# Gated spectral/MLP layer with gradients: two quarters of w1 loaded during the output pass into tiles of their own, and a new order of products where the gradient of x begins

## Chip, cores and metric

One core of a Trainium2 chip. The metric is the device time of one execution in microseconds (us), from the first to the last instruction and what lies around them; the median of several executions is compared. The layer has 2048 rows, model width D = 1024 and hidden width F = 3584, all in bf16.

## What is computed

The forward layer mixes a Fourier filter and an MLP with a squared ReLU by a gate for each row, and the call returns its output and the gradients of eight of its inputs:

```python
g = sigmoid((x * gate_w).sum(-1, keepdims=True))
a = irfft2(rfft2(x) * (w_r + 1j * w_i), s=(S, D))      # spectral branch
h = einsum("bsd,df->bsf", x, w1) + b1
r = where(h > 0, h, 0)
b = einsum("bsf,fd->bsd", r * r, w2) + b2              # MLP branch, fed from B_x
out = g * a + (1 - g) * b
out, vjp = jax.vjp(f, A_x, A_w_r, A_w_i, B_w1, B_b1, B_w2, B_b2, gate_w)
return (out, *vjp(grad_out))
```

The part that matters here is the last one. The output needs h2 = (relu h)² times w2. The kernel's second output is computed from dh (the gradient at the hidden layer) times the transpose of w1, plus the spectral and the gate's part of the gradient; the text calls it the gradient of x. Both are products of 2048 × 3584 by 3584 × 1024.

## The kernel before

The kernel runs in three stages: the hidden layer and its gradient (`mlp_in`), the gradients of w2 and w1 (`mlp_grads`), the output and gradient of x (`mlp_out`); the Fourier work is spread between the matmuls of the first stages. h2 and dh are kept transposed in DRAM scratch (`h2T_scr`, `dhT_scr`). All that follows is in `mlp_out`.

**Blocks and products.** `mlp_out` walks over NB = 8 blocks of 256 rows, first for the output ("h", from `h2T_scr`) and then for the gradient of x ("d", from `dhT_scr`). A block is loaded into the tile `even` or `odd` by its number, in two halves of the 28 chunks of 128 (`lo`: chunks 0 to 13, `hi`: 14 to 27). Apart from the first two blocks of "h", a block is multiplied by Strassen's scheme in Winograd's form: the block and the 3584 × 1024 matrix are cut in 2 × 2 quarters, and seven products take the place of eight. Each product (`p1` to `p7`) is a chain of 14 matmuls of 128 × 128 by 128 × 512 into one PSUM bank. The quarters of the block are a11, a21 (both in `lo`), a12, a22 (both in `hi`).

**The sums.** `Block.sums` makes four sums of a block's quarters on VectorE (S3 = a11 − a21; S1 = a21 + a22, in place of a21; S2 = S1 − a11; S4 = a12 − S2). `right` makes the four sums of the matrix's quarters (T1 = b12 − b11, T2 = b22 − T1, T4 = b21 − T2, T3 = b22 − b12), each over 128 × 7168 elements. The products need: p1 a11·b11, p2 a12·b21, p3 S4·b22, p4 a22·T4, p5 S1·T1, p6 S2·T2, p7 S3·T3. p1, p6, p7 and p4 follow one another in the bank X, each copied out by ScalarE before the next adds to it; p5 and p3 share the bank V.

**Where the matrices lie.** For "h" the quarters of w2 are in `w2L` (`cL`) and `w2R` (`cR`), T1, T2, T4 in the three tiles `wT1`, `wT2`, `wT4`, and T3 in place of `cR[:, lo]`. For "d" the quarters of w1 must be transposed: `quarter` issues seven DMA transposes from SyncE for one of them. One quarter has its own tile (`w1q`) and comes early. The other three are put where w2 lay: b12 in `cL[:, lo]`, b22 in `cL[:, hi]`, b21 in `wT2`; so each can start only when the last block of "h" is done with that place.

**What sets the order.** [...] Inside `mlp_out` the order on TensorE, VectorE and ScalarE is the order of the calls (`pe`, `dve` and `act` chain each instruction behind the one before). `ld` issues a DMA from SyncE's queue, `st` from GpSimd's; the scheduler sorts the two queues by when their work becomes due, and a DMA that has to wait for its buffer holds back all that stands behind it on its queue.

**Lines that the steps touch.** L1124 and L1163 allocate the rows of the incoming gradient and of x (3 buffers); L1145 and L1168 the scaled row `od`/`gd`; L1140 to L1153 are the tail of an output tile (`close`: add, then a product with a row sum, L1142, into `ot`; `put`: subtract and store); `prepare_x` (L1166) makes the spectral and gate part of a gradient tile and adds to `gacc`; L1318 to L1360 is the loop over blocks of "h"; L1363 to L1401 is the order where "d" begins; L1403 to L1422 the loop over its later blocks; L1423 to L1430 the end.

Of the kernel before, what the change touches and what calls it, by code (L numbers as in the profile page):

```python
# [10 lines left out]
P = 128  # L11
# [128 lines left out]
def kernel(  # L140
# [667 lines left out]

    def column_sums(sb_pool, acc, tag):

        tr_ = sb_pool.tile([P, D], FP32, name="tr_", tag=tag, bufs=1)
        nc.vector.transpose(out=tr_[:], in_=acc[:])
        part = sb_pool.tile([P, 32], FP32, name="part", tag="part")
        nc.vector.reduce_sum(out=part[:], in_=tr_[:].rearrange("p (b r) -> p b r", r=32), axis=mybir.AxisListType.X)
        return part

    def sums_out(sb_pool, ps_pool, tag, part, dst, bufs=2):

        pr = ps_pool.tile([32, 32], FP32, name="prow", tag=tag, bufs=bufs)
        mm(pr[:], lhsT=part[:], rhs=sel[:], start=True, stop=True)  # L820
        row = sb_pool.tile([32, 32], BF16, name="row", tag="row")
        nc.vector.tensor_copy(out=row[:], in_=pr[:])
        st(out=dst.rearrange("(b c) -> b c", c=32), in_=row[:])


    def mlp_grads():
# [255 lines left out]
    def mlp_out():  # L1082
# [4 lines left out]
        wp, wps = pool("w1p")  # L1087
        q0 = wp.tile([P, KH, H], BF16, name="w1q", tag="w1q")
        wb, wbs = pool("m3")
# [5 lines left out]
        row = lambda name, dt=FP16, bufs=2, tag=None: wb.tile([P, D], dt, name=name, tag=tag or name, bufs=bufs)  # L1095
        a_, go, na, v, cu, od, ot, blks = ({} for _ in range(8))
        B, Bx = {}, {}
# [25 lines left out]
        def fetch_g(t):  # L1123
            go[t] = row("go3", BF16, 3)  # L1124
            (ld if t < NT - 2 else st)(out=go[t][:], in_=go_perm[t])

# [10 lines left out]
        def close(t):  # L1137
            c_ = slice(t, t + 1)
            d_, g_ = cu.pop(t), go.pop(t)
            ot[t] = row("ot", BF16)  # L1140
            dve(V(out=d_[:], in0=d_[:], in1=v.pop(t)[:], op=ALU.add))
            dve(nc.vector.tensor_tensor_reduce(  # L1142
                out=ot[t][:], in0=d_[:], in1=g_[:], scale=1.0, scalar=0.0,
                op0=ALU.mult, op1=ALU.add, accum_out=bGo[:, c_],
            ))  # L1145
            od[t] = row("od", bufs=1)
            act(nc.scalar.mul(out=od[t][:], in_=d_[:], mul=omg[:, c_]))
            dve(STT(out=dsc[:, c_], in0=bGo[:, c_], scalar=-1.0, in1=gpg[:, c_], op0=ALU.mult, op1=ALU.mult))

        def put(t):  # L1150
            o_ = ot.pop(t)
            dve(V(out=o_[:], in0=od.pop(t)[:], in1=na.pop(t)[:], op=ALU.subtract))
            st(out=o0_perm[t], in_=o_[:])  # L1153


        gacc = None

        def fetch_xa(t):
            a_[t] = row("gx", FDT, tag="a_")
            (st if t < 4 else ld)(out=a_[t][:], in_=ax_scr[1][t][:])  # L1160

        def fetch_xo(t):
            go[t] = row("xo", BF16, 3, "go3")  # L1163
            (st if t < 4 else ld)(out=go[t][:], in_=x_perm[t])

        def prepare_x(t):  # L1166
            c_ = slice(t, t + 1)
            na[t], v[t], gd = row("gy", tag="na"), row("g1", tag="v", bufs=2), row("gd", tag="od", bufs=1)  # L1168
            act(nc.scalar.mul(out=na[t][:], in_=a_.pop(t)[:], mul=YS))
            act(nc.scalar.mul(out=gd[:], in_=gatew_bc, mul=dsc[:, c_]))  # L1170
            dve(V(out=v[t][:], in0=na.pop(t)[:], in1=gd[:], op=ALU.add))
            xo = go.pop(t)
            if t == 0:
                dve(nc.vector.tensor_scalar(out=gacc[:], in0=xo[:], scalar1=dsc[:, c_], scalar2=None, op0=ALU.mult))
            else:
                dve(STT(out=gacc[:], in0=xo[:], scalar=dsc[:, c_], in1=gacc[:], op0=ALU.mult, op1=ALU.add))

# [5 lines left out]
        class Block:  # L1183
# [31 lines left out]

            def kept(self, name, bufs):
                t_ = wb.tile([P, H], FP32, name=name, tag=name, bufs=bufs)
                act(nc.scalar.copy(out=t_[:], in_=self.X[:]))
                return t_

            def add(self, r, cols, acc, other):
                dve(V(out=fresh(2 * self.k + r)[:, cols], in0=acc[:], in1=other[:], op=ALU.add))  # L1222

            def p1(self):
                self.X = self.bank("pX")
                self.chain(self.X, self.a11, self.B["11"], True)
                self.c1 = self.kept("c1", 2)

# [21 lines left out]
            def p4(self):  # L1250
                self.chain(self.X, self.a22, self.B["T4"], False)
                act(nc.scalar.copy(out=fresh(2 * self.k + 1)[:, L], in_=self.X[:]))
                self.done(2 * self.k + 1)

            def p3(self):
                self.chain(self.V, self.S[4], self.B["22"], False)
                self.add(0, R, self.V, self.u2)
                self.done(2 * self.k)

        def right(dst, x, y):  # L1260
            dve(V(out=dst, in0=x, in1=y, op=ALU.subtract))  # L1261
# [49 lines left out]
        more, mores = pool("mpsz", "left", PSUM)  # L1311
        gacc = wb.tile([P, D], FP32, name="gacc", tag="gacc")
        wq = iter(())
        a, b = None, Block("h", N0)
        b.sums(3, 1, 2)
        for _ in made:
            pass
        for k in range(N0, NB):  # L1318
            last = k == NB - 1
            if k == N0 + 1:  # L1320
                wq = quarter(q0, 0, 0)
            b.p1()
            if a is None:
                put(2 * k - 1)
                load("h", k + 1)
            if last:
                for _ in quarter(cL[:, lo], 0, 1):
                    pass
            next(wq, None)
            b.p2()  # L1330
            next(wq, None)
            if a is not None:
                a.p4()
                load(*(("d", 0, st) if last else ("h", k + 1)))
            next(wq, None)
            b.p6()
            if a is not None:
                put(2 * k - 1)
            if last:
                for _ in quarter(cL[:, hi], 1, 1):  # L1340
                    pass
            next(wq, None)
# [8 lines left out]
            prepare(2 * k + 1), prepare(2 * k)  # L1351
            if last:
                fetch_xa(0), fetch_xa(1), fetch_xo(0)
            else:
                fetch_a(2 * k + 2), fetch_a(2 * k + 3)
# [7 lines left out]
        T1, T2, T4 = later["T"]  # L1363
        b11, b12, b21, b22 = q0[:], cL[:, lo], T2.bitcast(BF16), cL[:, hi]
        Bx.update({"11": b11, "21": b21, "22": b22, "T1": T1, "T2": T4, "T3": fp16(b12), "T4": fp16(cR[:, lo])})
        a.p4()
        load("d", 1, st)
        for _ in quarter(b21, 1, 0):
            pass
        put(2 * NB - 1)  # L1370
        a.p3()
        fetch_xo(1)
        x0, x1 = b, Block("d", 1)
        x0.p1()
        put(2 * NB - 2)
        right(Bx["T1"], b12, b11)
        x0.p5(True)
        prepare_x(0)
        x0.sums(4)
        x1.sums(3, 1, third=fp16(cR[:, hi])[:, :, 0:P])  # L1380
        x1.p1()
        prepare_x(1)
        fetch_xa(2), fetch_xo(2), fetch_xa(3), fetch_xo(3)
        x1.p5(True)
        right(Bx["T2"], b22, Bx["T1"])
        x0.p6()
        right(Bx["T3"], b22, b12)
        x1.sums(2)
        x0.p7()
        x1.p6()  # L1390
        x1.p7()
        right(Bx["T4"], b21, Bx["T2"])
        x0.p2("pZ")
        x0.p3()
        x0.p4()
        load("d", 2)
        prepare_x(2)
        x1.sums(4)
        x1.p2("pZ")
        prepare_x(3)  # L1400
        fetch_xa(4), fetch_xo(4), fetch_xa(5), fetch_xo(5)  # L1401
        a, b = x1, None
        for k in range(2, NB):  # L1403
            last = k == NB - 1
            b = Block("d", k)
            b.sums(3, 1, 2)
            b.p1()
            b.p2()
            a.p4()
            if not last:  # L1410
                load("d", k + 1)
            b.p6()
            a.p3()
            b.p5()
            b.sums(4)
            prepare_x(2 * k), prepare_x(2 * k + 1)
            if not last:
                fetch_xa(2 * k + 2), fetch_xo(2 * k + 2), fetch_xa(2 * k + 3), fetch_xo(2 * k + 3)
            if last:
                part = column_sums(wb, gacc, "tr_")  # L1420
            b.p7()
            a = b  # L1422
        pr = more.tile([P, H], FP32, name="prow", tag="pZ", bufs=2)  # L1423
        mm(pr[0:32, 0:32], lhsT=part[:], rhs=sel[:], start=True, stop=True)
        row_ = wb.tile([32, 32], BF16, name="row", tag="row")
        nc.vector.tensor_copy(out=row_[:], in_=pr[0:32, 0:32])
        st(out=out_8.rearrange("(b c) -> b c", c=32), in_=row_[:])
        a.done = lambda t: close_x(t, ld)
# [208 lines left out]
```

## Time and profile before

| what | us |
|---|---|
| median of 5 runs | 1272.23 |
| lowest and highest run | 1265.56, 1278.14 |
| the run that was profiled | 1265.56 |
| its span, first to last instruction | 1263.8 |
| TensorE busy | 1215.1 (96% of the span) |
| VectorE, ScalarE, GpSimd busy | 768.1, 622.3, 382.2 |
| TensorE busy from 1060 to 1080 us | 8.29 of 20 |
| TensorE busy from 1080 to 1100 us | 12.37 of 20 |
| TensorE busy from 1140 to 1160 us | 19.90 of 20 |

The last block of "h" ends and "d" begins at about 1055 us. Matmuls are pipelined and their ends are modelled, so busy time is not time at peak. The profile also tells the clock that TensorE was granted, as a share of the full one: 0.69 from 1060 to 1080 us, 0.76 from 1080 to 1100, and 1.00 in the stretches of 20 us from 860 to 1060. A line `A <- B` in the view of waits says that A's engine stood idle until B was done.

### The profile page before, as it was taken

Reading aid. Unit: us, or ns where it says so; the run is one execution under the profiler, and the core shown is the slowest. Engines: PE = TensorE matmul, PEld = TensorE weight load, DVE = VectorE, ACT = ScalarE, POOL = GpSimd, SP = SyncE. Lnnn points to the kernel's source line nnn. Section 1 sums busy time; section 2 is a strip of 40 time slices with the busy share of each in tenths; the row PEclk is TensorE's granted clock in tenths of the full one; section 3 lists DMA queues with packets and bytes.
Section 4 is the critical chain, followed back from the end, with each engine's and each line's share of the span. In section 5 each row is a group of like instructions: output and inputs, shape, how many; then the busy total and the mean of one; then the engine's idle time right before and its main releaser. Section 6 shows DMA issues by size and latency. Waiting matters only on the chain.

```text
span 1263.8 us, 18707 instructions
## 1 busy us (share of the span) xinstructions
PE 1215.1 (96%) x6535; PEld 589.5 (47%) x6656; DVE 768.1 (61%) x1734; ACT 622.3 (49%) x1128; POOL 382.2 (30%) x629
## 2 busy tenths in 40 slices
PE   8999999999999999999999999999999996699998
PEld 5555555544444444444444455555444443244443
DVE  3556456575888968767676245545485666555454
ACT  4657667744787762444445466666322323123232
POOL 0124424331545532333245566562000012000000
PEclk9999999998999999999999999999999998799999
DMA  9567575665676859899899899874944569946450
GB/s 285 187 192 194 141 194 164 178 174 131 191 201 195 208 159 209 167 195 242 206 166 284 180 263 250 202 191 143 280 129 137 155 175 191 220 120 185 137 163 34
DMA packets 325913, 234.36 MB, mean 185 GB/s; under 512 B 198220, under 2 KB 284394, under 8 KB 325818
## 3 DMA queue, kind: packets, MB, share of 16 engines
q1 hardware_dynamic: 293184, 136.21, 48.0%
q0 software_dynamic: 32432, 96.90, 24.8%
q8 instruction: 52, 0.85, 0.3%
q14 instruction: 43, 0.35, 0.1%
q10 hardware_dynamic: 202, 0.04, 0.0%
HBM read 107.24 MB, written 81.81 MB: 150 GB/s over the span
## 4 chain that ended last, share of the span: by engine, by line
PE 79%; DVE 5%; issue 4%; DMA 3%; ACT 1%; POOL 1%; SPq 0%; DVEq 0%; POOLq 0%
PE pw L1045 15%; PE ph L724 13%; PE pd L734 12%; PE pX L1208 11%; PE pV L1208 8%; PE pX L917 6%; PE pV L917 4%; PE acc L1295 4%; DMA out_dram<-ot 1%; PE pui L309 1%; PE pu L309 1%; PE pki L562 1%; PE px L413 1%; PE pk L276 1%; PE pv L444 1%
## 5 line engine op out<-in xcount | busy, mean ns | idle before, releaser
L724 PE MATMUL ph<-xT,w1g 128*128 128x512 bf16 x865 | 216.2, 381 | 3.2 <-DMA w1g<-in_B_w_dram 1.2
L734 PE MATMUL pd<-dbT,w2T 128*128 128x512 bf16 x875 | 211.7, 382 | 0.9
L738 DVE SCALAR_TENSOR_TENSOR dhT<-pd,rT 128x512 bf16<-128x512 f32 x112 | 77.0, 688 | 103.8 <-PE pd L734 95.4
L734 PEld LDWEIGHTS <-w2T 128*128 128x128 bf16 x896 | 87.4, 98 | 103.3 <-issue 2.2
L1045 PEld LDWEIGHTS <-res 128*128 128x128 bf16 x896 | 86.0, 98 | 97.1
L724 PEld LDWEIGHTS <-w1g 128*128 128x128 bf16 x896 | 85.2, 98 | 93.8 <-DMA w1g<-in_B_w_dram 1.5
L1045 PE MATMUL pw<-odd,res 128*128 128x512 bf16 x496 | 112.6, 379 | 0.8
L726 ACT ACTIVATE rT<-ph,b1col 128x512 bf16<-128x512 f32 x112 | 77.1, 688 | 65.1 <-PE ph L724 64.9
L1208 PEld LDWEIGHTS <-dS 128*128 128x128 f16 x574 | 56.6, 99 | 79.1 <-DVE wT L1261 8.1
L225 POOL DMA_DIRECT2D z_scr<-u x96 | 58.5, 616 | 107.5 <-ACT u L293 52.8
L1045 PE MATMUL pw<-even,res 128*128 128x512 bf16 x374 | 84.5, 379 | 0.5
L416 ACT CAST x<-px 64x512 f16<-64x512 f32 x128 | 74.1, 579 | 18.4 <-PE px L413 17.3
L1047 ACT CAST wo<-pw 128x512 bf16<-128x512 f32 x56 | 32.6, 585 | 82.0 <-PE pw L1045 80.1
L727 ACT ACTIVATE h2T<-rT 128x512 bf16<-128x512 bf16 x112 | 70.5, 630 | 2.3
L225 POOL DMA_DIRECT2D r<-y_scr x96 | 58.2, 611 | 40.1 <-ACT re L549 23.3
L1208 PEld LDWEIGHTS <-even 128*128 128x128 bf16 (+1 forms) x392 | 38.8, 99 | 61.7 <-issue 16.8
L1208 PEld LDWEIGHTS <-odd 128*128 128x128 bf16 (+1 forms) x392 | 38.2, 98 | 47.8 <-issue 1.9
L1222 DVE TENSOR_TENSOR cu<-pV,u 128x512 f16<-128x512 f32 x28 | 19.3, 690 | 62.6 <-PE pV L1208 43.8
L1208 PE MATMUL pX<-wT,dS 128*128 128x512 f16 x196 | 47.5, 397 | 7.7 <-DVE wT L1261 7.6
L1181 POOL DMA_DIRECT2D out_dram<-gxo x14 | 7.6, 541 | 152.7 <-DVE gxo L1180 152.7
L917 PEld LDWEIGHTS <-S 128*128 128x128 f16 x336 | 32.4, 98 | 45.4 <-DVE S L904 7.2
L453 POOL DMA_DIRECT2D y_scr<-pc x64 | 35.8, 561 | 51.0 <-DVE pc L450 36.1
(250 smaller groups left out, 2237.2 us busy)
## 6 DMA issues: line engine op xcount, KB each, us to landing
h2T_scr<-h2T POOLq DMA_DIRECT2D x28, 512.0 KB, 4.5
dhT_scr<-dhT POOLq DMA_DIRECT2D x28, 512.0 KB, 5.7
z<-z_scr SPq DMA_DIRECT2D x64, 128.0 KB, 3.1
y_scr<-pc POOLq DMA_DIRECT2D x64, 128.0 KB, 4.2
ax_scr<-yo POOLq DMA_DIRECT2D x32, 256.0 KB, 4.6
w1g<-in_B_w_dram SPq DMA_DIRECT2D x14, 512.0 KB, 4.7
out_dram<-wo POOLq DMA_DIRECT2D x56, 128.0 KB, 5.4
even<-h2T_scr SPq DMA_DIRECT2D x8, 896.0 KB, 5.6
```

The lines of the kernel that those rows point to most:

```text
L225: issue(out=a, in_=b) if stored else issue(out=b, in_=a)
L416: nc.scalar.copy(out=x[lanes[n], c, :, 0:HW], in_=px[lanes[c], n])
L453: st(out=y_scr[:][c, :, :, h].rearrange("r x t l -> (r x) t l"), in_=pc[:, n])
L724: mm(ph[:], lhsT=w1g[:, dc, fc % 2 * P : (fc % 2 + 1) * P], rhs=xT[:, dc, ss], start=(dc == 0), stop=(dc == DC - 1))
L726: nc.scalar.activation(rT[:], ph[:], ACT.Relu, bias=b1col[:, fc : fc + 1])
L727: nc.scalar.activation(h2T, rT[:], ACT.Square)
L734: mm(pd[:], lhsT=w_[:, ec, fc % FGC * P : (fc % FGC + 1) * P], rhs=dbT[:, ec, ss], start=(ec == 0), stop=(ec == DC - 1),)
L738: return STT(out=dhT, in0=pd[:], scalar=2.0, in1=rT[:], op0=ALU.mult, op1=ALU.mult, accum_out=gb1part[:, fc, sb : sb + 1],)
L917: self.mm = mm(acc[:], lhsT=lhs[:, t, c_], rhs=rhs[:, t, :], start=start and t == 0, stop=t == KH - 1, skip_group_check=True,)
L1045: mm(pw[:], lhsT=xr[:, t, d_ * P : (d_ + 1) * P], rhs=cur[:, t, :], start=(t == 0), stop=(t == NT - 1))
L1208: pe(mm(acc[:], lhsT=lhs[:, c, :], rhs=rhs[:, c, :], start=start and c == 0, stop=c == KH - 1, skip_group_check=True,))
L1295: turn["PE"] = mm(acc[:], lhsT=blks["h", k][:, c, t2 * P : (t2 + 1) * P], rhs=w_[:, c, :], start=(c == 0), stop=(c == FC - 1))
```

## The change

- A second quarter of w1 (b12) gets a tile of its own, `w1q1`. Its seven transposes follow those of the first quarter, from the second block of the Strassen loop on, on SyncE's queue.
- The other two are loaded into `w2L` when the last block of "h" leaves it: b22 into `lo`, b21 into `hi`. Nothing is loaded into `wT2` any more; T1, T2 and T4 stay in `wT1`, `wT2`, `wT4`, and T3 replaces b12 in its tile.
- Space for it comes from other buffers: two instead of three for the rows of the incoming gradient and of x, one instead of two for the copy of p1 (`c1`), the row `od`/`gd` moves to a free end of the tile `even`, and the sum `gacc`, the third sum of the second block, one copy of p1 and the end's small tiles move to the place of w2's T3.
- All loads of "d" are issued from SyncE; before, those of its first two blocks and tiles were issued from GpSimd.
- Where "d" begins: the first product of its block 0 stands ahead of the last two of "h". T1 and T2 are made between the tails of the last two output tiles, T3 after them and T4 later. The order of products of the first two blocks and the place of the rows' preparation are new; the third product of block 1 is in it too, and the loop leaves it out.
- A tile of the gradient is closed when the second of its halves is done, whichever it is.
- At the end, the transpose and reduction of `gacc` stand in VectorE's chain ahead of the last addition of p7, and the small matmul that ends it stands in TensorE's chain ahead of the last p4.

```diff
-        q0 = wp.tile([P, KH, H], BF16, name="w1q", tag="w1q")
+        q0, q1 = (wp.tile([P, KH, H], BF16, name=f"w1q{j}", tag=f"w1q{j}")[:] for j in range(2))
...
+        scaled = later["even"][:, FC * BW : FC * BW + D].bitcast(FP16)
...
-            go[t] = row("go3", BF16, 3)
-            (ld if t < NT - 2 else st)(out=go[t][:], in_=go_perm[t])
+            go[t] = row("go3", BF16)
+            ld(out=go[t][:], in_=go_perm[t])
...
+        aside = cR.rearrange("p c e -> p (c e)")
...
-            (st if t < 4 else ld)(out=a_[t][:], in_=ax_scr[1][t][:])
+            ld(out=a_[t][:], in_=ax_scr[1][t][:])
...
+            def half(self, t):
+                halves[t] = halves.get(t, 0) + 1
+                if halves[t] == 2:
+                    halves[t] = 0
+                    self.done(t)
...
+        def both():
+            yield from quarter(q0, 0, 0)
+            yield from quarter(q1, 0, 1)
...
-                wq = quarter(q0, 0, 0)
+                wq = both()
...
-            if last:
-                for _ in quarter(cL[:, lo], 0, 1):
-                    pass
...
-                load(*(("d", 0, st) if last else ("h", k + 1)))
+                load(*(("d", 0) if last else ("h", k + 1)))
+            if last:
+                for _ in quarter(cL[:, lo], 1, 1):
+                    pass
...
-                for _ in quarter(cL[:, hi], 1, 1):
-                    pass
...
-        b11, b12, b21, b22 = q0[:], cL[:, lo], T2.bitcast(BF16), cL[:, hi]
-        Bx.update({"11": b11, "21": b21, "22": b22, "T1": T1, "T2": T4, "T3": fp16(b12), "T4": fp16(cR[:, lo])})
+        b12, b21, b22 = q1, cL[:, hi], cL[:, lo]
+        Bx.update({"11": q0, "21": b21, "22": b22, "T1": T1, "T2": T2, "T3": fp16(b12), "T4": T4})
+        x0 = b
+        x0.p1()
+        right(T1, b12, q0)
         a.p4()
-        load("d", 1, st)
+        load("d", 1)
         for _ in quarter(b21, 1, 0):
             pass
+        right(T2, b22, T1)
         put(2 * NB - 1)
         a.p3()
-        fetch_xo(1)
-        x0, x1 = b, Block("d", 1)
-        x0.p1()
         put(2 * NB - 2)
-        right(Bx["T1"], b12, b11)
         x0.p5(True)
-        prepare_x(0)
+        right(Bx["T3"], b22, b12)
         x0.sums(4)
-        x1.sums(3, 1, third=fp16(cR[:, hi])[:, :, 0:P])
-        x1.p1()
...
+        x0.p6()
+        for t in range(2):
+            fetch_xa(t), fetch_xo(t)
+        x1 = Block("d", 1)
+        x1.sums(3, 1, third=third)
+        x1.p1(second)
+        x1.sums(2)
         x1.p5(True)
...
         x0.p7()
         x1.p6()
-        x1.p7()
-        right(Bx["T4"], b21, Bx["T2"])
+        x1.sums(4)
+        right(T4, b21, T2)
+        x0.p3()
+        prepare_x(0)
         x0.p2("pZ")
-        x0.p3()
+        prepare_x(1)
         x0.p4()
         load("d", 2)
...
+        x1.p7()
+        x1.p2("pZ")
         prepare_x(2)
-        x1.sums(4)
-        x1.p2("pZ")
+        x1.p3()
...
-            a.p3()
+            if k > 2:
+                a.p3()
...
-                part = column_sums(wb, gacc, "tr_")
+                dve(nc.vector.transpose(out=turned_, in_=gacc))
+                rows_ = turned_.rearrange("p (b r) -> p b r", r=32)
+                dve(nc.vector.reduce_sum(out=part, in_=rows_, axis=mybir.AxisListType.X))
...
-        mm(pr[0:32, 0:32], lhsT=part[:], rhs=sel[:], start=True, stop=True)
+        pe(mm(pr[0:32, 0:32], lhsT=part, rhs=sel[:], start=True, stop=True))
```

## The prediction, made before the changed kernel ran

> **What bounds the kernel now.** First the page: how busy TensorE is, and where it isn't.
>
> ```profile
> span 1263.8 us, 18707 instructions
> PE 1215.1 (96%) x6535; PEld 589.5 (47%) x6656; DVE 768.1 (61%) x1734; ACT 622.3 (49%) x1128; POOL 382.2 (30%) x629
> ...
> PE   8999999999999999999999999999999996699998
> ...
> PEclk9999999998999999999999999999999998799999
> ```
>
> TensorE (PE) is the bound nearly everywhere; one hole lies in slices 34 and 35 (of 31.6 us), where the gradient of x begins and where the clock drops too. The view of TensorE's waits from 1050 to 1130 us names what it stood for:
>
> ```profile
> PE pV L1208 <- DVE wT L1261: 11.7, 1, 11.7
> PE pX L1208 <- DVE wT L1261: 7.6, 1, 7.6
> PE pX L1208 <- ACT u L1218: 2.0, 3, 0.7
> ```
>
> Two sums of w1's quarters on VectorE (DVE) came late. VectorE's timeline and the chain that ended last show why:
>
> ```profile
> 1071.26 1.22 DVE L1142 CUSTOM_DVE_ANT_0 ot<-cu,go 128x1024 bf16<-128x1024 f16 x1 [7.08 <-DMA out_dram<-ot]
> ...
> 1073.20 3.88 DVE L1261 TENSOR_TENSOR wT<-w2L,w1q 128x7168 f16<-128x7168 bf16 x1
> ...
> 1092.08 3.89 DVE L1261 TENSOR_TENSOR wT<-w2L,wT 128x7168 f16<-128x7168 bf16 x1 [2.12 <-DMA w2L<-in_B_w_dram]
> ```
>
> ```profile
> 1054.36 16.74 DMA out_dram<-ot
> ```
>
> T1 stood behind the tail of an output tile, which waited for a store that took 16.74 us to land; T2 waited for the transposed quarter b22. Both are slow DMAs. SyncE's queue (SPq):
>
> ```profile
> 1034.90 53.39 SPq L180 DMA_TRANSPOSE w2L<-in_B_w_dram  x14
> 1088.64 9.87 SPq L180 DMA_TRANSPOSE wT<-in_B_w_dram  x7
> ```
>
> Beside GpSimd's loads of dh, 14 transposes took 53.39 us (3.8 each); after them, seven took 9.87 (1.4 each).
>
> From 1055.42 (end of the last block's p7) to 1124.92 (first product of block 2) run 14 products. At the undisturbed 3.02 us each that is 42.3 us; it took 69.5. So 27.2 us are lost: waits of 11.7 + 7.6 + 2.0, and some 5 by the clock (p5 held TensorE from 1077.14 to 1082.25, 2.1 over 3.02; p6 from 1096.03 to 1102.10, 3.0 over). That is the most that the change can win.
>
> **The change part by part.** I follow the changed order with the durations above, from the same 1055.42, where p7 of block 7 ends in both.
>
> *Loads.* Seven transposes (b12) leave the hole; they stand about 905 us behind the first seven, which took 12.6 us there from 893.18. At 1.4 each they add 9.8 us to SyncE's queue. Behind them stand the halves of block 2 of "h", issued at 906.4 before; first needed by TensorE at 932.25. A shift of 10 us plus about 6 to land ends at 922: hidden by some 10 us, and dearer only beyond that. In the hole the queue is now: first half of block 0 of "d" (issued about 1031.2, when p5 of block 6 is done), two small rows, nine transposes, second half of block 0, a gradient row, five transposes, a gradient row, block 1 with two rows of the spectral part between its halves. The first transpose can start at 1034.90 as before. Nine at 1.4 and one store beside them (1 us) end about 1049. The second half then lands as such loads do from SyncE, not as from GpSimd (last number: us from issue to landing):
>
> ```profile
> odd<-dhT_scr POOLq DMA_DIRECT2D x2, 896.0 KB, 15.8
> ...
> even<-dhT_scr SPq DMA_DIRECT2D x1, 896.0 KB, 6.8
> ```
>
> So it lands about 1056; S1 of block 0 needs it at 1057.96. Five more transposes end near 1058 (b21 is needed after 1090), block 1 is in by 1066 and 1069 (its second half waits for the moved p4, 1061.5). These rows of the forecast are the least certain: both ends below.
>
> *A rule that speaks against this.* The Trainium skill (DMA: Bandwidth & Descriptors, Issuing engines are not separate DMA queues) says that DMAs from different issuers run on the same 16 engines and interleave, so the issuer alone should not change a rate. By that rule the transposes keep their 3.8 us: nine end at 1069, the half lands at 1076, everything behind is 18 us late, and the change loses. By the trace, transposes ran at 1.4 us with other loads of SyncE in front and behind, and at 3.8 only among GpSimd's 4096-byte packets; those are gone but for the stores. I take 1.4, and keep 3.8 as the rival.
>
> *Products.* p1 of block 0 needs only the first half and b11: 1055.42 to 1058.44. It also fills the gap of 0.67 in which p4 waited for ScalarE's copy. p4 and p3 of block 7 follow to 1064.5. VectorE: S3, S1, S2 of block 0 end at 1060.1 as before, then T1 (3.88) to 1063.98: p5 runs without a wait, 1064.5 to 1067.5. Then the tail of tile 15 (1.9), T2 (3.88) to 1069.85: p6 waits **2.3**. p1 of block 1 ends at 1076.0. VectorE goes on: store's subtraction, addition for p3, tail of tile 14 (0.6 + 0.7 + 0.7 + 1.3 and 0.7 for ScalarE's scaled row), subtraction 0.6, T3 3.88 (to 1078.3), S4, third and S1 of block 1 (3 × 1.05): p5 of block 1 starts at 1081.6, a wait of **5.5**. Then p7, p6, p3, p2 need nothing late. T4 needs S4 of block 1 in front of it, whose single buffer is free only when p3 of block 0 ends; 1.1 + 3.88 after that, while p2 covers 3.02: p4 waits **2.0**. p7, p2, p3 of block 1 follow.
>
> *Clock.* After the waits of 11.7 and 7.6 us the granted clock was 0.50, and rose in the 1081:1082 and 1101:1102 rows:
>
> ```profile
> 1067.00:1068.00 1.00, 0.00 (x0) 0.00 (x0) 0.00 (x0) 0.00 (x0) 0.00 (x0) 0.87 1.07 300
> ...
> 1081.00:1082.00 1.00, 1.00 (x5) 0.40 (x4) 0.48 (x1) 0.00 (x0) 0.00 (x0) 0.80 1.55 156
> ...
> 1101.00:1102.00 1.00, 1.00 (x3) 0.29 (x2) 0.00 (x0) 0.00 (x0) 0.00 (x0) 0.56 0.94 242
> ```
>
> TensorE had stopped at about 1065.5 and the clock fell at 1067.7, 2.3 us later. For the wait of 5.5 I take **2.4**, between the measured 2.1 and 3.0. The skill's page TensorE: Matmul & The Clock Gate (Part 1) has the half rate come after an idle window of about 3.4 us. By the rule waits of 2.3 and 2.65 us (below) are free of it; by the row one may lower the clock, for up to 3 us. The first costs nothing either way (VectorE sets the next start); for the last I take 0 and keep 3 for the range.
>
> Sum: 2.3 + 5.5 + 2.0 + 2.4 = 12.2 us lost in place of 27.2: **−15.0 us**. (15 products now run before block 2 instead of 14; the loop leaves that one out.)
>
> *The end.* The last lines of VectorE and TensorE before:
>
> ```profile
> 1251.98 1.25 DVE L812 STREAM_TRANSPOSE tr__12730<-gacc 128x1024 f32<-128x1024 f32 x1
> ...
> 1253.72 1.20 DVE L814 TENSOR_REDUCE part<-tr__12730 128x32 f32<-128x1024 f32 x1
> ...
> 1254.97 0.25 PE L1424 MATMUL prow<-sel,part 128*32 128x32 f32 x2 [0.16 <-DVE part L814]
> ```
>
> Ten matmuls of p4 ran ahead of the small matmul. Now it stands ahead of all: TensorE is idle from 1251.85 until the reduction is done, 1251.98 + 1.25 + 1.2 = 1254.45 (0.6 earlier, as the addition moves behind it), then 0.25 and all of p4 and p3. p4 ends at 1257.8 in place of 1256.2, p3 too: **+1.6 us**.
>
> *Costed at nothing.* Two buffers for the rows: each load waits one tile longer, but its user is an iteration (21.15 us) away and the load takes 3.5 to 5 us; the block halves behind it on the queue move by under 2 us (one addition to `gacc`, 1.28, and a start), with some 5 us to spare (second half issued at 1176.32, lands by 1183.5, first needed near 1188.5). If that cover went, each of 6 iterations would pay the excess. The single c1 is free 15 us before its next writer; `od` was single before. Steady blocks stay at seven products of 3.02.
>
> Together −15.0 + 1.6 = **−13.4 us**: 1265.56 becomes 1252.2 for a profile like this one. That run is the lowest of the five; against their median 1272.23 it is **1259**.
>
> **The rivals.**
>
> *The clock stays up, or VectorE's waits are shorter:* p6's wait may already lower the clock, and then the slower p6 and p1 fill the 5.5 us wait and TensorE resumes warm. Gain 15.8 to 17: 1255.5.
>
> *Some transposes are slow:* three stores still come from GpSimd in this stretch, and single transposes took 5.1 us at 1037.70 and 1045.62. Two such put the half at 1063.5, 5.5 after its need; VectorE's chain moves by that: gain 8, 1264.
>
> *Slower:* the queue is first in, first out, and one place decides: the second half of block 0 behind nine transposes. At 3.8 us each it lands at 1076, 18 us after 1057.96, and 18 − 13.4 makes +4.5: 1277. It decides from 3.3 us a transpose (half landing at 1071.4). For: the mean of the 14 was 3.8. Against: the 4096-byte packets beside them are gone.
>
> *The change doesn't do what it says:* the added transposes at 905 could delay "h" as much as they save; the 10 us of cover speak against it, and the gain would be some 8 at the worst of that.
>
> **How the numbers follow.** Forecast 0.55 (1255 to 1263 with the clock and the end's 3 us), warmer 0.18, some slow transposes or late middle 0.18, the slower case 0.09. This kernel's measurement can tell about 1% (12.7 us, so 1259.5). Below that lie 0.36 of the forecast's 0.55 and all of 0.18: faster 0.54. Slower by over 1% (over 1285) needs transposes beyond 4.9 us: 0.05. The rest is 0.41. The range 1250 to 1268 takes in the first three cases, the scatter of the runs before, and leaves out the last.
>
> **What would show it.** TensorE's waits: two sums (T2, T4) near 2 us, S1 of block 1 near 5.5, none for T1; about 0.5 clock for 4 to 6 us once; 14 transposes into w2L in about 20 us; block 2's p1 near 1113; the small matmul waiting 2.6 at the end. Wrong would be: a wait on a dh load longer than 2 us, transposes over 2.5 us, or a hole before 1050.

## The result, and the profile after

| | before | changed |
|---|---|---|
| median of all runs | 1271.52 (75 runs, 1253.24 to 1289.82) | 1252.58 (38 runs, 1247.24 to 1263.37) |
| median of the runs compared (next paragraph) | 1267.80 (38 runs) | 1252.58 (38 runs) |
| the profiled run, its span | 1265.56, 1263.8 | 1250.13, 1248.4 |
| mean granted clock of the profiled run | 0.987 | 0.994 |

The ratio is 0.9901, with a 95% interval of 0.9884 to 0.9917, so the change gains about 1%. This ratio, and all medians and ratios below, are of fast runs: those over 1.5% above their kernel's fastest are left out, about half of the runs before and none of the changed kernel's. Two later sets of runs of the changed kernel gave medians of 1253.48 and 1253.57.

The page of the changed kernel, busy time and slices as before:

```profile
span 1248.4 us, 18680 instructions
PE 1212.5 (97%) x6535; PEld 588.4 (47%) x6656; DVE 766.1 (61%) x1734; ACT 622.1 (50%) x1128; POOL 372.8 (30%) x615
...
PE   8999999999999999999999999999999999899997
...
PEclk9999999999999999999999999999999999899999
```

The two slices with 6 have become one with 8. TensorE did nearly the same busy time (1212.5 in place of 1215.1) in a span 15.4 us shorter. What it still waited for, in the view of waits from 1050 to 1130 us:

```profile
PE pX L1196 <- DVE wT L1256: 4.3, 2, 2.4
PE pV L1196 <- DVE odd L1192: 3.0, 1, 3.0
```

T1 is no longer in it, nor a transfer. SyncE's queue, and the view of transfers from 1030 to 1075 us (last number: us to landing):

```profile
1030.26 13.38 SPq L180 DMA_TRANSPOSE w2L<-in_B_w_dram  x9
1043.74 0.53 SPq L1095 DMA_DIRECT2D even<-dhT_scr  x1
...
1047.69 9.80 SPq L180 DMA_TRANSPOSE w2L<-in_B_w_dram  x5
```

```profile
even<-dhT_scr SPq DMA_DIRECT2D x2, 896.0 KB, 8.1
odd<-dhT_scr SPq DMA_DIRECT2D x2, 896.0 KB, 7.0
out_dram<-ot POOLq DMA_DIRECT2D x4, 256.0 KB, 5.5
```

Fourteen transposes took 13.38 + 9.80 = 23.2 us where they had taken 53.39, and a store lands in 5.5 us instead of 12.4 to 16.7. TensorE's timeline at the three places that wait, and at the end (start, duration, then what ended the idle time before):

```profile
1065.40 4.88 PE L1196 MATMUL pX<-wT,dS 128*128 128x512 f16 x14 [2.37 <-DVE wT L1256]
...
1076.32 4.66 PE L1196 MATMUL pV<-wT,odd 128*128 128x512 f16 x14 [3.02 <-DVE odd L1192]
...
1095.03 4.87 PE L1196 MATMUL pX<-wT,even 128*128 128x512 f16 x14 [1.97 <-DVE wT L1256]
...
1229.68 3.19 PE L1196 MATMUL pX<-w1q,dS 128*128 128x512 f16 x14
1235.57 0.25 PE L1425 MATMUL prow<-sel,w2R 128*32 128x32 f32 x2 [2.71 <-DVE w2R L1421]
1235.75 4.88 PE L1196 MATMUL pX<-wT,odd 128*128 128x512 f16 x14
```

In order these are p6 of block 0, p5 of block 1, p4 of block 0, the last p7, the small matmul and the last p4. Behind each of the four waits the product lasts 4.7 to 4.9 us instead of 3.19: the granted clock was 0.5 for 3.4 us of it, although no wait is longer than 3.0 us.

**Where the 15.4 us between the two spans came from.** From the end of the last block's p7 to the first product of block 2: before 1055.42 to 1124.75, 14 products, 27.0 us lost at 3.02 each; changed 1050.78 to 1108.81, 15 products, 12.7 us lost (58.0 − 45.3). That gives 14.3. From the start of the last p7 to the end of the span: 15.2 before, 18.7 changed, which takes 3.6 back. The remaining 4.6 us lie ahead of 1050 us: the profiled run before had an interval of half clock from 289.5 to 296.3 us, and the changed one had none there. This differs between runs of one kernel. Of the fourteen profiles of this study ten have one or two windows of 3.4 us at half clock at that place (among them two of the changed kernel's three), and in those of the changed kernel and its variants block 0's first product starts anywhere from 1050.8 to 1062.7 us, with up to 4 us of waits at L562 and up to 3.2 at L413. So profiles are compared below by the hole and by the end, not by their spans. Between the two, from block 2's first product to the last p7, 40 products took 120.9 us, 3.02 each as before.

### The profile page after: what moved, and what is told of

It reads as the page before. It is cut to its first block, busy times and chain, and to the rows that moved or that the text cites. A ratio compares the mean times of both kernels' runs of the same rounds, so it can differ in the third digit from the quotient of the medians.

```text
span 1248.4 us, 18680 instructions
## 1 busy us (share of the span) xinstructions
PE 1212.5 (97%) x6535; PEld 588.4 (47%) x6656; DVE 766.1 (61%) x1734; ACT 622.1 (50%) x1128; POOL 372.8 (30%) x615
## 3 DMA queue, kind: packets, MB, share of 16 engines
q0 software_dynamic: 30672, 90.61, 23.6%
## 4 chain that ended last, share of the span: by engine, by line
PE 82%; DVE 6%; issue 3%; ACT 1%; DVEq 0%
PE pw L1028 15%; PE ph L724 12%; PE pX L1196 12%; PE pd L734 12%; PE pV L1196 9%; PE pX L900 7%; PE pV L900 5%; PE acc L1290 4%; PE pui L309 1%; PE pu L309 1%; PE pki L562 1%; PE px L413 1%; PE pk L276 1%; PE pv L444 1%; DVE even L1542 1%
## 5 line engine op out<-in xcount | busy, mean ns | idle before, releaser
L1136 POOL DMA_DIRECT2D out_dram<-ot x16 | 8.6, 540 | 171.5 <-DVE ot L1135 159.6
```

## The experiments

All lost times are measured in the same way: from the end of the last p7 of "h" to the first product of x block 2, less 3.02 us a product. "End" is from the start of the last p7 to the end of the span.

| kernel | median us (runs) | ratio to before, 95% | lost in the hole | end |
|---|---|---|---|---|
| before, in the three sets of runs | 1264.94 (37), 1272.06 (7), 1269.81 (20) | | 27.0 | 15.2 |
| changed, three profiles | 1252.58, 1253.48, 1253.57 | 0.9901, 0.9929, 0.9875 | 12.7, 12.1, 11.2 | 18.7, 18.6, 17.0 |
| before, loads from SyncE | 1261.95 (20) | 0.9973 (0.9945 to 1.0) | 20.7 | 16.4 |
| changed, loads of the first x blocks from GpSimd | 1255.34 (18) | 0.9938 (0.9898 to 0.9979) | 16.2 | 20.1 |
| changed, only the rows from GpSimd | 1254.71 (4) | 0.9888 (0.9818 to 0.9958) | 12.4 | 18.8 |
| changed, second quarter late | 1258.73 (20) | 0.9936 (0.9908 to 0.9965) | 16.0 | 17.2 |
| changed, products in the old order | 1264.29 (22) | 0.9962 (0.9934 to 0.9989) | 17.5 | 17.0 |
| changed, another order | 1246.7 (4) | 0.9809 (0.9745 to 0.9872) | 1.0 | 18.7 |
| changed, unread products in the waits | 1249.55 (4) | 0.9836 (0.9761 to 0.9911) | 9.6 | 17.0 |
| changed, small matmul later | 1249.95 (4) | 0.9851 (0.9784 to 0.9919) | 11.3 | 15.4 |
| another order and small matmul later | 1237.71 (6) | 0.977 (0.9708 to 0.9831) | 1.0 | 15.4 |

The kernel before shows how far sets can differ, so times are best compared within a set. The first set, on one chip, has the changed kernel (1253.48), loads from GpSimd, the kernel before with SyncE, and the late quarter. The second, on another chip, has the other order, the unread products, the later small matmul, and both edits together; no run of the changed kernel is in it, and gains there are taken against the 1252.6 to 1253.6 of the others. The third, on the second set's chip, has the changed kernel (1253.57), the old order, the rows from GpSimd, and both edits again.

**Who issues the loads.** The control:

> The changed kernel once more, beside the next three. Every theory: TensorE waits of about 2.4, 3.0, 2.0 us where the gradient of x begins and 2.7 us near the end, as in its first profile; 15 products between the last p7 of the output and block 2 lose 12 to 13 us.

Measured: 1253.48 us, waits of 2.57, 4.70 and 1.97 us in the hole and 2.71 at the end, 12.1 us lost. Then both directions of the same edit. In the changed kernel, back to GpSimd:

```diff
-        load("d", 1)
+        load("d", 1, st)
```

(the same for block 0 of "d", for the rows of `fetch_g`'s last two tiles, and for the first four of `fetch_xa` and `fetch_xo`).

> The changed kernel with the first loads for the gradient of x (blocks 0 and 1, the rows of tiles 0 to 3, the last two gradient rows) issued from GpSimd again, as before the change. Theory A (GpSimd's packets slow the transposes): the 14 transposes take 35 us or more instead of 23, stores of output tiles land late again, and the kernel loses 6 to 12 us against the changed one. Theory B (the early second quarter and the new order are what counts; who issues a load does not matter): within 3 us of the changed kernel.

And in the kernel before, the same loads from SyncE:

```diff
-        load("d", 1, st)
+        load("d", 1)
```

> The kernel before, with these same loads issued from SyncE and nothing else changed. Theory A: the transposes run at about 1.4 us, no store takes over 8 us to land, T1 waits only for VectorE's order (about 5 us of TensorE's wait instead of 11.7), and 10 to 14 us of the gain come from this alone. Theory B: at most 3 us faster than before.

SyncE's queue and VectorE's waits of the changed kernel with GpSimd's loads, and VectorE's waits of the kernel before with SyncE's:

```profile
1034.66 54.12 SPq L180 DMA_TRANSPOSE w2L<-in_B_w_dram  x14
```

```profile
DVE odd L1192 <- DMA odd<-dhT_scr: 4.7, 1, 4.7
```

```profile
DVE odd L1204 <- DMA odd<-dhT_scr: 6.4, 1, 6.4
DVE gacc L1176 <- DMA xo<-in_A_x_dram: 3.6, 1, 3.6
```

With the loads on GpSimd the transposes are as slow as they ever were (54.12 us for 14), as theory A had it. Yet the time follows theory B: the hole loses only 4.1 us more than the control (16.2 against 12.1), and the median is 2 us higher. In the new order T1 needs none of those fourteen, T2 and T3 the first seven and T4, after 1090, the last seven, so what is felt is one half of block 1 that lands late, and S1 of block 1 behind it.

In the kernel before, the issuer alone takes the loss from 27.0 to 20.7. TensorE's wait for T1 falls from 11.7 to 4.9, as expected, and T2 has no wait for b22; but T2 still starts at 1091.84 (1092.08 before), because ahead of it VectorE has stood 6.4 us for a half of block 1 and 3.6 for a row of x, which now come late on SyncE. So the 10 to 14 us that I had expected of the issuer there are 6.3 in the hole, and 5.1 with the end. The time says no more: 0.9973, with an interval that reaches 1.0, and 3.0 us between the medians.

To see which loads slow the transposes, only the rows (256 KB) went back to GpSimd, and the halves (896 KB) stayed on SyncE:

> The changed kernel with the rows of grad_out, x and the spectral part issued from GpSimd in the hole as in the kernel before, the halves of the x blocks from SyncE. Theory (it is the 4096-byte packets of the software queue, rows or halves, that slow the transposes): the nine transposes take over 25 us instead of 13.4 to 13.9, the half of block 0 behind them lands late, a wait on a load of dh appears, median 1256 to 1264. Rival (only the large halves do it): the transposes stay at 1.5 to 2 us each, no new wait, median 1252 to 1255.

```profile
1038.44 14.23 SPq L180 DMA_TRANSPOSE w2L<-in_B_w_dram  x9
...
1053.37 12.38 SPq L180 DMA_TRANSPOSE w2L<-in_B_w_dram  x5
```

The rival holds in the main: 1.6 us a transpose for the nine, 2.5 for the five (it had said 1.5 to 2), no new wait. The packets of GpSimd's queue are about as large (3.15 MB in 960 packets, against 7.08 MB in 2000 before), so packets of this size are not enough by themselves. What differs is how much of the engines' time that queue takes: in the view of transfers from 1030 to 1085 us, 15.0% here against 55.6% before and 52.3% with the halves on GpSimd. That the share is the cause, and not the size of the single transfer (256 KB or 896 KB), is not shown: both went together.

**The early quarter.** b12's transposes held back until the last block of "h":

```diff
         def both():
             yield from quarter(q0, 0, 0)
-            yield from quarter(q1, 0, 1)
...
             b.p1()
+            if last:
+                for _ in quarter(q1, 0, 1, turn["PE"]):
+                    pass
```

(the fourth argument makes the transposes wait for the latest instruction of TensorE, that block's p1.)

> The changed kernel with the second quarter's seven transposes held back until the last output block has done its first product, so that 21 transposes stand in this stretch again. Theory A: at 1.4 us each they are nearly all in time; the last gradient rows and the second half of block 1 come some 3 us late: 2 to 5 us slower than the changed kernel. Theory B (the early quarter is the gain): 10 us slower or more.

Measured: 5.2 us over the control's median, just over the 2 to 5 of theory A, and 3.9 more lost in the hole. It shows where: on SyncE's queue seven more transposes stand ahead of block 1's second half, and VectorE waits for it.

```profile
1083.61 1.09 DVE L1192 TENSOR_TENSOR odd<-odd 128x1792 f16<-128x1792 bf16 x1 [4.60 <-DMA odd<-dhT_scr]
```

**The order.** The changed kernel with its loads and buffers, but the products and sums of the first two x blocks as in the kernel before (T1 behind the tails of the last two output tiles, T2 after p5 of block 1, T3 after p6, `prepare_x` early):

```diff
-        x0.p1()
-        right(T1, b12, q0)
         a.p4()
...
+        x0.p1()
         put(2 * NB - 2)
...
+        right(T1, b12, q0)
         x0.p5(True)
+        prepare_x(0)
...
+        x1.p5(True)
+        right(T2, b22, T1)
+        x0.p6()
+        right(Bx["T3"], b22, b12)
```

> The changed kernel (early quarter, loads from SyncE, buffers as in it) with the products and sums of the first two x blocks in the order of the kernel before. Theory (the early quarter and the loads from SyncE gave most of the gain, the new order little): T1 still waits for the tails of the last two output tiles, so p5 waits 4 to 6 us, but T2 and T4 wait for no load; 7 to 10 us lost besides the two or three waits of 0.7 for ScalarE, median 1251 to 1256, equal to the changed kernel within 3 us. Rival (the new order is what fills the hole): 15 us or more lost, median 1258 to 1264.

It gave 1264.29 us, beside the changed kernel's 1253.57 on the same chip, and lost 17.5 us in the hole against 11.2. TensorE's waits:

```profile
PE pV L1196 <- DVE wT L1256: 5.0, 1, 5.0
PE pV L1196 <- DVE dS L1192: 2.6, 1, 2.6
PE pV L1196 <- DVE odd L1192: 2.0, 1, 2.0
PE pX L1196 <- ACT u L1206: 2.0, 3, 0.7
PE pX L1196 <- DVE wT L1256: 1.5, 1, 1.5
```

The first wait came as the theory had it (T1 behind the tails), but four more stand behind it: my theory that the order gave little fell, and the rival holds. Read as a chain, the issuer takes the hole from 27.0 to 20.7, the early quarter (with its buffers) to 17.5, the order to 11.2 to 12.7. The steps depend on one another: in the new order the issuer is worth 4.1 us and the early quarter 3.9. In time the order is the largest step: without it the ratio is 0.9962, little below the 0.9973 of the issuer alone (in another set), and with it 0.9875 in the same set. Between those two medians lie 10.7 us, more than the 5 to 6 of the profiles; the profiled run without the order, 1258.16, is the second lowest of its 22, so an ordinary one may lose more. No trace shows where.

Then the order was taken further, on the reading that VectorE works without a gap and only does things in the wrong sequence:

```diff
         x0.p5(True)
-        right(Bx["T3"], b22, b12)
-        x0.sums(4)
-        x0.p6()
+        x0.p2("pZ")
...
         x1 = Block("d", 1)
         x1.sums(3, 1, third=third)
+        right(Bx["T3"], b22, b12)
+        x0.p6()
         x1.p1(second)
+        x0.sums(4)
         x1.sums(2)
         x1.p5(True)
         x0.p7()
+        right(T4, b21, T2)
         x1.p6()
-        x1.sums(4)
-        right(T4, b21, T2)
+        prepare_x(0)
         x0.p3()
-        prepare_x(0)
-        x0.p2("pZ")
+        x1.sums(4)
         prepare_x(1)
```

> The changed kernel with another order where the gradient of x begins: p2 of the first x block right behind its p5, the sums of the second x block (with S1) ahead of T3, T4 behind p7 of the first x block, the second block's S4 later. Same work. Theory (VectorE works without a gap from 1057 to 1082 us and what TensorE waits for is only late in its order): the three waits of 2.4 to 2.6, 3.0 to 4.7 and 2.0 us shrink to 1 us together or less and the clock stays up; the hole (first product of the x blocks to the first of the third x block, 15 products at 3.02 us) goes from 57.4 to 58.0 us to 46 to 48, median 1241 to 1244. Rival (VectorE as a whole is the bound there, not its order): the waits move to other products and the hole keeps over 54 us, median over 1249.

```profile
PE pX L1196 <- DVE w1q L1256: 0.6, 1, 0.6
```

That is the only wait left: p2 of block 0, which needs none of the sums, covers T2; S1 of block 1 no longer stands behind T3; T4 is made while p6 and p3 run. What still waits 0.6 us is p7, for T3. The hole shrank to 46.3 us for 15 products, 1.0 lost: the order was the bound, not VectorE as a whole. The median, 1246.7, is 2.7 us above what I expected: its profiled run lost 4.0 us at L562 and started block 0 at 1059.47, and it has only four runs.

**The clock.** Products that nobody reads fill the four waits:

```diff
+        def filler(n):
+            f_ = more.tile([P, H], FP32, name="fill", tag="pZ", bufs=2)
+            for _ in range(n):
+                pe(mm(f_[:], lhsT=q0[:, 0, 0:P], rhs=q0[:, 1, :], start=True, stop=True))
...
+        filler(9)
         x0.p6()
```

> The changed kernel with products that nobody reads (9, 12, 7 and 10 matmuls of 512 columns) on TensorE in front of the four products that wait, so that it works through the waits. Theory (idleness of 2 us and more lowers the clock): no granted clock of 0.5 in the hole nor at the tail, the four products at 3.02 to 3.2 us, waits named as before but shorter by the fillers' time, median 1247 to 1250 (3 to 6 us less, 1.7 for each drop that goes). Rival (the clock falls for another reason, as at 290 us where TensorE does not wait): drops of 3.4 us stay at the same places, median 1252.5 to 1254.5.

```profile
1066.84 2.10 PE L1365 MATMUL fill<-w1q 128*128 128x512 bf16 x9
1069.37 3.19 PE L1196 MATMUL pX<-wT,dS 128*128 128x512 f16 x14 [0.43 <-DVE wT L1256]
...
1080.30 3.19 PE L1196 MATMUL pV<-wT,odd 128*128 128x512 f16 x14 [2.12 <-DVE odd L1192]
```

All four products are back at 3.19, no half clock is left in the hole or at the end, and the median is 3 to 4 us below the changed kernel's, with more work on TensorE. So idleness lowers the clock. But p5 kept its full clock behind a wait of 2.12 us, where p4 of the profile after lost it behind 1.97; the last section says why.

**The end.** The last p4 goes ahead of the small matmul, and the transpose and sum of `gacc` behind p7's addition:

```diff
+            b.p7()
             if last:
                 dve(nc.vector.transpose(out=turned_, in_=gacc))
...
-            b.p7()
             a = b
+        a.done = lambda t: close_x(t, ld)
+        a.p4()
         pr = more.tile([P, H], FP32, name="prow", tag="pZ", bufs=2)
...
-        a.done = lambda t: close_x(t, ld)
-        a.p4()
         a.p3()
```

> The changed kernel; after the last p7 only the last addition moves: the transpose and row sum of gacc come after that product's addition, and the small matmul into prow goes between the last p4 and p3 instead of ahead of p4. Theory (a wait of 2.7 us in front of prow also lowers the clock under p4): p4 follows p7 at once, no wait named, its duration 3.2 us instead of 4.7 to 4.9, from the start of the last p7 to the end of the span 14.5 to 15.5 us (before 15.16, changed 18.72): 2.7 + 1.7 = 4.4 us less, median 1248 to 1249.5. Rival (the tail hides the small products some other way, the end is set by the last store): the wait goes, and the end moves by less than 1 us, median 1252 to 1254.

```profile
1238.26 3.18 PE L1196 MATMUL pX<-wT,odd 128*128 128x512 f16 x14 [0.68 <-ACT u L1206]
1241.39 0.25 PE L1427 MATMUL prow<-sel,w2R 128*32 128x32 f32 x2
1241.57 3.20 PE L1196 MATMUL pV<-w2L,dS 128*128 128x512 bf16 x14
```

The end takes 15.4 us. ScalarE's copy, which I had forgotten, still makes p4 wait 0.68. The median, from four runs, is 3.5 us under the changed kernel's.

**Both.** The other order and the moved small matmul together, in the second and the third set:

> Both edits, the new order at the start of the gradient of x and the moved small matmul at the end. If they lie apart on the path, the gains add: 10 + 4.4 us, median 1237 to 1240, ratio to the kernel before near 0.975. If the end is set by something else than TensorE (the last stores), no more than the order alone.

> The changed kernel once more, beside the next ones on the same chip: 1252 to 1254 us median, hole (first product of the x blocks to the first of the third x block) 57 to 58 us.

> The new order at the start of the gradient of x and the moved small matmul at the end, timed beside the changed kernel. By the two edits alone (11 us in the hole, 3.3 to 4.4 at the end) 1238 to 1242, 12 to 15 us under the changed kernel. If the first four runs (one of 1247.8 among three of 1237 to 1240) hold the true spread, the median comes to 1242 or more.

The second set gave 1239.23 us (four runs), the third 1237.71 (six) beside the changed kernel's 1253.57: 15.9 us less, a little more than expected, and 0.977 (0.9708 to 0.9831) of the kernel before. The page of the third set's profile:

```profile
span 1235.5 us, 18681 instructions
PE 1208.5 (98%) x6536; PEld 588.2 (48%) x6656; DVE 767.9 (62%) x1734; ACT 622.0 (50%) x1128; POOL 372.9 (30%) x615
...
PE   9999999999999999999999999999999999999998
```

The second set's profiled run took 1247.78, with two intervals of half clock at 684 and 858 us and its waits ahead of the hole: the scatter in front stays.

## Why the prediction was right, and where it was off

The time, 1252.58, lies in the range, and the mechanism held: TensorE no longer waits for T1, the transposes run fast, and the waits that remain are those that were named. In the hole two terms were mis-sized, and that they nearly cancel is luck; the end was mis-sized too.

- **Transposes.** Taken at 1.4 us each, measured 1.49 for the nine and 1.96 for the five; the half behind the nine landed after 7.7 us where 6.8 was taken, and no dh load made anybody wait (in the control VectorE waited 0.24 us for it). The slower rival's price (3.8 us) came true when the halves of the x blocks went back to GpSimd, though not in the place that the rival named, since the half then no longer stands behind the transposes. Its cause was named too narrowly: packets of that size did little harm while that queue took 15% of the engines' time.
- **The DMA rule.** The Trainium skill (DMA: Bandwidth & Descriptors, Issuing engines are not separate DMA queues) says that DMAs of all issuers interleave on the same 16 engines, and the prediction drew from it that the issuer should not change a rate. Here the transposes took 1.5 to 2.0 or 3.9 us by who issued the halves. The measurement decides, and the choice of 1.4 was right.
- **T2's old wait.** The prediction put it to b22. In the kernel before, b22 held T2 for the last 2.1 us only; ahead of that VectorE had stood 6.6 us in `prepare_x`, for a row of ScalarE's:

```profile
1088.08 0.69 DVE L1171 TENSOR_TENSOR g<-gy,gd 128x1024 f16<-128x1024 f16 x1 [6.59 <-ACT gd L1170]
```

```profile
1085.47 0.58 ACT L1218 COPY c<-pX 128x512 f32<-128x512 f32 x1 [11.00 <-PE pX L1208]
```

  That row stood in ScalarE's order behind the copy of block 1's p1, which was late because p5 ahead of it had waited for T1. So fast transposes alone could bring T2 forward by 2 us at most, and with the loads from SyncE they gave 0.2 (1091.84 instead of 1092.08). The new order, which makes T2 ahead of `prepare_x`, did. The hole before is 27.0 us, not 27.2: block 2 begins at 1124.75, where the prediction read 1124.92.
- **Loads at 905 us, and what was costed at nothing.** No new wait appeared ahead of the hole: the view of waits names the same 1.8 us in the "h" blocks in both kernels. The later blocks of "d" lost nothing either (3.02 us a product).
- **T1, T2, T4.** No wait, 2.3 and 2.0 predicted; none, 2.37 and 1.97 measured.
- **S1 of block 1.** 5.5 predicted, 3.0 measured in the profile after; 4.7 in the control:

```profile
1081.38 5.51 PE L1196 MATMUL pV<-wT,odd 128*128 128x512 f16 x14 [4.70 <-DVE odd L1192]
```

  The term was sized for a p6 at full clock. In the profile after p6 ran at half clock and took 1.7 us of the wait with it; in the control it kept its clock and p5 waited 4.7. That is the rival in which p6's wait lowers the clock already. But TensorE did not resume warm from it: p5 was slow in both.
- **Clock in the hole.** 2.4 us for one drop; it was three drops of one interval each, under p6, p5 and p4, with 1.7, 1.5 and 1.7 us over 3.19. Waits and clock together lost 12.7 where 12.2 was predicted: the waits were 2.4 us shorter than forecast (7.4 for 9.8) and the clock cost 2.5 us more (4.9 for 2.4), two errors that cancel.
- **The end.** This step failed in size: +1.6 predicted, +3.6 measured. The wait was 2.71, as foreseen; the clock was taken at 0 with 3 as the bound, and fell in five of the eight profiles that have this end, for 1.5 us and more each. Where it didn't, the end is 17.0 to 17.2, or +1.8 to 2.1, close to the +1.6.
- **The level.** For a profile like the one before, 1252.2 was forecast and 1250.1 came. But 4.6 us of that fall lie ahead of 1050 us, where the three profiles of the changed kernel differ among themselves (block 0 starts at 1050.8, 1055.6 and 1052.6); the two stages that were costed gave −10.7 (−14.3 and +3.6) of the −13.4. For the median, −13.4 was set against 1272.23, the median of the first five runs, which gave 1259. Against 1267.80 it gives 1254.4, and 1252.58 came, so the miss of 6 us was mostly in the starting level.

## What to carry to other kernels

Take the loss at a hand-over between two loops apart by the last releaser of each wait, then ask of each waiting product whether another that needs nothing new can stand in front of it: here that was worth nearly as much as the whole change (27.0 to 12.7 us lost, then 1.0). Look at what runs beside transposes: here four loads of 896 KB, with the rows, issued from GpSimd took fourteen of them from 23.6 to 54.1 us. And don't put a small product with a late operand in front of a long one in TensorE's order when it can go behind.

## What the runs showed of the hardware

**The clock is decided on a fixed grid.** In all 14 traces the intervals of half clock begin and end at whole multiples of 3.413 us from one another, apart from the end of the last, which the end of the execution cuts. The Trainium skill (TensorE: Matmul & The Clock Gate, Part 1) gives this very window, 3413 ns and free-running. For the fall its table of states asks for at least one idle window; in these runs less was enough. Cut on its own grid, the profile after shows, from 1062 us on (window; its length, TensorE's busy time; after the brackets the granted clock, DMA's share, GB/s):

```profile
1062.24:1065.65 3.41, 1.04 (x6) 0.32 (x5) 3.41 (x2) 0.00 (x0) 0.00 (x0) 1.00 1.11 323
1065.65:1069.07 3.42, 3.42 (x10) 1.18 (x9) 3.32 (x7) 1.15 (x1) 0.54 (x1) 0.50 1.17 312
...
1092.96:1096.38 3.42, 1.45 (x8) 0.64 (x8) 3.42 (x4) 0.17 (x1) 0.00 (x0) 1.00 0.00 0
1096.38:1099.79 3.41, 3.41 (x10) 1.22 (x9) 3.38 (x5) 0.98 (x1) 0.54 (x1) 0.50 0.31 105
```

and the control, where the same wait for T2 (2.57 us) fell across a boundary:

```profile
1065.62:1069.03 3.41, 2.27 (x11) 0.83 (x9) 3.33 (x4) 0.56 (x1) 0.00 (x0) 1.00 1.09 306
1069.03:1072.44 3.41, 1.98 (x10) 0.92 (x11) 3.34 (x5) 0.02 (x1) 0.54 (x1) 1.00 1.14 324
1072.44:1075.86 3.42, 3.37 (x16) 1.52 (x16) 3.38 (x5) 1.72 (x2) 0.54 (x1) 1.00 1.17 309
```

I cut every trace so from 1050 us on, with TensorE's idle time from the starts and modelled ends of its matmuls. Of some 760 windows at full clock, all 22 with 2.05 us or more of idle time were followed by a window at half clock, none of those with 1.95 or less, and one of the two with 1.97. Of 36 windows at half clock, the 23 with at most 0.42 us idle were followed by full clock and the 13 with 0.65 or more by another at half clock. Half clock does half the work in the same busy time (p6 of the kernel before, nearly all at half clock, took 6.06 us in place of 3.19), so both bounds mean nearly one thing: about 1.4 to 1.5 us of full-speed work in a window (3.41 − 1.97 = 1.44; half of 3.41 − 0.42 is 1.50, half of 3.41 − 0.65 is 1.38). So a wait of some 2 to 3.9 us (twice 1.97, for one cut in half by a boundary) may or may not lower the clock, as it falls inside a window or across a boundary. That changes from run to run: the wait of 2.7 us at the end lowered it in five profiles and not in three. If it falls, it costs 1.5 us and more.
